# Value products of a head pair in one go from the second batch on, and the fifth chunk of the products with U on four column tiles

## The chip, the cores and the metric

The kernel runs on one core of a Trainium2 chip. A core has a matrix engine (TensorE; PE in the profile, with its loads of the stationary operand shown apart as PEld), a vector engine (VectorE, DVE), a scalar engine (ScalarE, ACT), GpSimd (POOL) and SyncE (SP), which here starts most transfers. The metric is the device time of one execution in microseconds (us), lower is better; the time quoted is the median of several executions.

## What is computed

Attention that keeps only the scores within tau of a row's largest, then a channel mixing block with a low-rank mixing along the sequence, then a mixture of eight experts. The part that the change touches is the value product of the attention and the low-rank mixing:

```python
batch, n_heads, seq, head_dim = 4, 8, 576, 64
scores = scale * np.matmul(q, k.transpose(0, 1, 3, 2))
attn = masked_softmax(scores, tau)
out = np.matmul(attn, v)                 # value products
...
xt = x.transpose(0, 2, 1)                # (batch, 512, 576)
h = xt @ U @ V                           # U: 576 x 32, V: 32 x 576
u = x + h.transpose(0, 2, 1)
ch = np.maximum(u @ w_ch1, 0.0) @ w_ch2
x = u + ch                               # then gating and experts
```

## The kernel before

The four batches (b = 0 to 3) go one after another. In each, the eight heads are taken as four pairs (hp = 0 to 3), and the 576 query rows of a pair as five groups (g = 0 to 4): groups 0 to 3 are 128 rows of both heads, group 4 is the last 64 rows of both. `front` makes the scores of a group, their maxima, exponentials, mask and norm; `back` turns the group's probabilities round with PE transposes into PSUM tiles `tp` (L416, L422), which ACT copies to `ptt` (L417, L423, L424). Batch 0 runs alone (`attention_alone`). From batch 1 on the attention of batch b is interleaved with the channel block of batch b-1 (`channel`, whose matmuls are lines L698 to L700 and L713 to L715), by cost numbers that the generators yield. These only order the code: a list scheduler of the framework then sets the order of each engine by priority and by when it believes operands and buffers to be ready.

The 576 query rows of a pair have two halves: columns 0 to 255 (groups 0 and 1) and 256 to 575 (groups 2 to 4), each with its own `ptt`. The value products of a half write one PSUM tile `po`: four pairs of matmuls with 64 stationary columns each, L435 for the first head into the upper 64 partitions and L436 for the second into the lower 64, and then one matmul with 128 stationary columns, L439, for the last key chunk of both heads. They stand in `back` behind group 1 for the first half and behind group 4 for the second. ACT copies `po` to `xT` (L442), and a chain of small steps is appended, `chain`: transposes of that half into chunks (`tx`, L461), copies of the chunks to `xsd` (L463 by DVE; the fifth chunk, 64 rows, by ACT in L472, or L475 in batch 0), and, for the second half alone, the products with U (`tT`, L484), a replication (L490) and the products with V (L499 or L506). The products with U are five matmuls, one for each chunk, with 32 stationary columns each. Chunk c writes partitions 32·(c mod 4) on, so that chunks 0 to 3 lie on four column tiles of the array, and chunk 4 lies on the first one again.

All matmuls whose operands are plain float32 run as two passes, and the trace shows both. From batch 1 on the PSUM tag `tp` has two buffers, which `tp`, `po`, `tx`, `tT` and the tiles after them share (`po_tile`); scores have two buffers of their own (`s`) and the channel block two (`mm`).

A stretch, below, is a run of matmuls on PE with fewer than 128 stationary columns (L435 and L436, L484, and the gating logits L751), between matmuls with the whole width. Transposes with a 64-partition output are not among them. In the program's order for PE there are 76 stretches before: 40 of value products, 26 of products with U and 10 of logits.

Of the kernel before, what the change touches and what calls it, by code (L numbers as in the profile page):

```python
# [14 lines left out]
AF = mybir.ActivationFunctionType  # L15
# [32 lines left out]
HALVES = ((0, 256), (256, 320))  # L48
# [35 lines left out]
SCALED = 1  # L84
# [19 lines left out]
def attention_channel_moe(ctx, tc, qk, vv, tau, umat, vrep, wch, wgl, wexp, consts, out):  # L104
    nc = tc.nc
    pe, dve, act, pool, sp = nc.tensor, nc.vector, nc.scalar, nc.gpsimd, nc.sync
# [11 lines left out]
    u_sb = cp.tile([128, 5 * RK], F32, name="u_sb")  # L118
# [30 lines left out]
    def bank(tag, shape, name):  # L149
        return BANKS["pool"].tile(shape, F32, tag=tag, name=name, bufs=BANKS["bufs"][tag])  # L150
# [17 lines left out]
    def po_tile(name):  # L168
        return bank("po" if "po" in BANKS["bufs"] else "tp", [128, 512], name)
# [81 lines left out]
    u_flat, u_sb = u_sb, u_sb.rearrange("p (c r) -> p c r", c=5)  # L251
# [143 lines left out]
    def back(b, hp, g, inp, G):  # L395
        pt, rvs = G.pt, G.rvs
        nm = f"{b}_{hp}_{g}"
        last = g == 4
        v = inp[3]
        src = pt.rearrange("p a b -> p (a b)")  # L400
        half = g // 2 if g < 4 else 1
        o, n = HALVES[half]
        if g in (0, 2):
            if half == 0 and b == 0 and hp % 2:

                PT[0] = mlp.tile([128, 9, n], F32, tag="yT1", name=f"ptt{nm}")
            else:
                PT[0] = ap.tile([128, 9, n], F32, tag=f"ptt{half}", name=f"ptt{nm}", bufs=1)
        ptt = PT[0]
        q0 = g * 128 - o  # L410
        if not last:
            for c0 in range(0, 9, 4):
                m = min(4, 9 - c0)
                tp = bank("tp", [128, 4, 128], f"tp{nm}_{c0}")
                for c in range(c0, c0 + m):
                    pe.transpose(tp[:, c - c0], src[:, c * 128:c * 128 + 128], ident)  # L416
                act.activation(ptt[:, c0:c0 + m, q0:q0 + 128], tp[:, :m], AF.Copy)  # L417
                yield 0.11 * m
        else:
            tp = bank("tp", [128, 4, 128], f"tp{nm}")  # L420
            for c in range(4):
                pe.transpose(tp[:, c], src[:, c * 128:c * 128 + 128], ident)  # L422
            act.activation(ptt[:, 0:4, 256:320], tp[:, :, :64], AF.Copy)  # L423
            act.activation(ptt[:, 5:9, 256:320], tp[:, :, 64:], AF.Copy)  # L424
            tp = bank("tp", [128, 2, 128], f"tpr{nm}")
            pe.transpose(tp[:64, 0], src[:, 512:576], ident)
            pe.transpose(tp[:, 1], src[:, 448:576], ident)
            act.activation(ptt[:64, 4, 256:320], tp[:64, 0, :64], AF.Copy)
            act.activation(ptt[64:, 4, 256:320], tp[64:, 1, 64:], AF.Copy)
            yield 0.65  # L430
        if g not in (1, 4):
            return
        po = po_tile(f"po{nm}")
        for j in range(4):
            pe.matmul(po[:64, :n], lhsT=v[:, j * 64:j * 64 + 64], rhs=ptt[:, j], start=(j == 0), stop=False)  # L435
            pe.matmul(po[64:, :n], lhsT=v[:, 384 + j * 64:448 + j * 64], rhs=ptt[:, 5 + j], start=(j == 0), stop=False)  # L436
            if b == 0:
                yield 0.6
        pe.matmul(po[:, :n], lhsT=v[:, 256:384], rhs=ptt[:, 4], start=False, stop=True)  # L439
        xT = rows_of(b)  # L440
        xu = xT[:, hp, o:o + n]
        act.activation(xu, po[:, :n], AF.Copy)  # L442
        CHAIN.append(chain(nm, hp, half, xT, xu, rvs if b < SCALED else None))
        if b:
            yield 2.4

    def chain(nm, hp, half, xT, xu, rvs):

        o, n = HALVES[half]
# [4 lines left out]
        xsd = XS[0]  # L454
# [24 lines left out]
            next(conv)  # L479
        pst = po_tile(f"tT{nm}")[:, :128]  # L480

        for c in range(5):
            r = 32 * (c % 4)
            pe.matmul(pst[r:r + 32], lhsT=u_sb[:, c], rhs=xsd[:, c], start=(c < 4), stop=(c not in (0,)))  # L484
        tT = ap.tile([128, 128], F32, tag="tT", name=f"tT{nm}", bufs=1)
        act.activation(tT, pst, AF.Copy)
        yield 0.7
# [19 lines left out]
            act.activation(u, pu[:, :n], AF.Copy)  # L507
            yield 0.45

    PT, XS, RV, CHAIN = [None], [None], [None], []  # L510

    def link():

# [13 lines left out]
    def rows_of(b):  # L527

        if b not in X:
            for _ in STORE.pop(b - 2, ()):  # L530
                pass
            X[b] = mlp.tile([128, 4, S], F32, tag=f"yT{b % 2}", name=f"yT{b}")
        return X[b]
# [354 lines left out]
    early, first, cap, jump, n1, base0, base1, most, key, pos, over, t1, t2 = (ex1[:, i] for i in range(13))  # L888
# [482 lines left out]
```

## Time and profile before

| | us |
|---|---|
| median of 3 runs | 1046.02 (1045.58 to 1048.26) |
| the profiled execution | 1037.89 |
| its span, first to last instruction | 1036.1 |
| PE busy in it | 1001.9 (97%) |
| DVE, ACT, POOL busy | 717.5, 625.4, 134.3 |

A row of the list of groups or of the timeline is: line, engine, operation, output tile, input tiles, shape and count. The start that the trace gives for a matmul is when its data begin to stream; its end lies after the start of the next one, since matmuls overlap in the pipeline. So what a matmul costs on PE is read from the distance of two starts, not from its duration. A share of busy time near 100% on PE says that hardly any time is left in which it waits; it does not say that the array works at its best in that time.

### The profile page before, as it was taken

The numbers are of one execution on the slowest core, as the hardware profiler recorded it, in microseconds if no ns is written. First come the engines' busy times: TensorE is split into PE (matmuls) and PEld (weight loads), VectorE is DVE, ScalarE is ACT, GpSimd is POOL, SyncE is SP. The second block draws the span as 40 slices with busy tenths as digits, with TensorE's granted clock in tenths as the row PEclk, the third lists the DMA queues.
The fourth block names the chain that finished last, engine by engine and source line by source line (L and its number), as shares of the span: only waits on it lengthen the run. The fifth ranks groups of instructions, "written<-read, shape, count | busy, mean of one in ns | idle before, by whom it ended". The sixth has DMA issues, their size and how long they took to land. (4 is left out here: it accounts for less than half of the span.)

```text
span 1036.1 us, 17665 instructions
## 1 busy us (share of the span) xinstructions
PE 1001.9 (97%) x6256; PEld 836.1 (81%) x6256; DVE 717.5 (69%) x1761; ACT 625.4 (60%) x1270; POOL 134.3 (13%) x115
## 2 busy tenths in 40 slices
PE   7898999999999999999999999999999999999996
PEld 4666677767677787788888898999998988889984
DVE  7988676877668878686776664583378855566673
ACT  6888877886677767767574653422354334455562
POOL 1331133231000000000000000004410321111100
PEclk9999999999999999999999999999999999999999
DMA  6745477865332322422121110354055565555650
GB/s 211 229 141 158 156 238 237 259 207 170 104 112 85 110 76 93 134 78 83 59 85 42 42 40 32 128 191 136 20 181 186 169 224 175 171 189 197 202 183 16
DMA packets 58241, 143.71 MB, mean 139 GB/s; under 512 B 7389, under 2 KB 8157, under 8 KB 58144
## 3 DMA queue, kind: packets, MB, share of 16 engines
q1 hardware_dynamic: 54784, 132.27, 39.1%
q0 software_dynamic: 3360, 10.23, 3.0%
q8 instruction: 51, 0.84, 0.3%
q14 instruction: 46, 0.38, 0.1%
HBM read 124.65 MB, written 18.61 MB: 138 GB/s over the span
## 5 line engine op out<-in xcount | busy, mean ns | idle before, releaser
L1121 ACT ACTIVATE eh<-ew 128x512 fp32r<-128x512 f32 x160 | 94.2, 628 | 68.1 <-PE el L1237 44.6
L1122 DVE TENSOR_TENSOR el<-ew,eh 128x512 fp32r<-128x512 f32 x160 | 106.3, 690 | 38.0 <-ACT eh L1121 36.6
L698 PE MATMUL l<-uh,w0h 128*128 128x256 f32 (+2 forms) x352 | 126.6, 360 | 0.7 <-ACT yT L507 0.7
L363 DVE SCALAR_TENSOR_TENSOR p<-s,st,p 128x576 f32<-128x576 f32 x144 | 114.2, 815 | 17.4 <-ACT p L359 13.7
L700 PE MATMUL l<-uh,w0l 128*128 128x256 f32 (+2 forms) x352 | 122.8, 349 | 0.0
L699 PE MATMUL l<-ul,w0h 128*128 128x256 f32 (+2 forms) x352 | 122.5, 348 | 0.0
L359 ACT ACTIVATE p<-s,st 128x576 f32<-128x576 f32 x144 | 103.7, 739 | 28.8 <-DVE st L348 27.5
L348 DVE TENSOR_REDUCE st<-s 128x1 f32<-128x576 f32 x144 | 105.4, 751 | 18.9 <-PE s L315 18.2
L713 PE MATMUL l<-hh,w1h 128*128 128x512 f32 (+3 forms) x320 | 115.5, 361 | 0.0
L714 PE MATMUL l<-hl,w1h 128*128 128x512 f32 (+3 forms) x320 | 113.0, 353 | 0.0
L715 PE MATMUL l<-hh,w1l 128*128 128x512 f32 (+3 forms) x320 | 112.5, 351 | 0.0
L417 ACT ACTIVATE ptt<-tp 128x512 f32<-128x512 f32 (+1 forms) x192 | 88.2, 491 | 30.3 <-PE tp L416 30.1
L313 PE MATMUL s<-kh,qs 128*128 128x288 f32 x320 | 95.2, 318 | 5.3 <-DVE p L363 3.6
L677 POOL TENSOR_TENSOR w1l<-wr,w1h 128x512 fp32r<-128x512 f32 x24 | 31.8, 1335 | 526.4 <-DVE rha L980 428.8
L416 PE MATMUL tp<-cst,p 128*128 128x128 f32 x576 | 91.1, 276 | 6.4 <-ACT ptt L417 6.3
L718 DVE TENSOR_TENSOR yT<-l,yT 128x448 f32<-128x448 f32 (+2 forms) x96 | 50.2, 523 | 59.3 <-PE l L715 58.5
L315 PE MATMUL s<-kl,qs 128*128 128x288 f32 x320 | 89.0, 298 | 0.0
L373 ACT ACTIVATE p<-p,rv 128x576 f32<-128x576 f32 x108 | 78.7, 772 | 15.5 <-DVE rv L380 15.5
L416 PEld LDWEIGHTS tp<-cst,p 128*128 128x128 f32 x576 | 67.6, 140 | 21.7 <-ACT ptt L417 12.8
L675 ACT ACTIVATE w1h<-wr 128x512 fp32r<-128x512 f32 x64 | 38.4, 628 | 60.9 <-PE l L714 56.6
L313 PEld LDWEIGHTS s<-kh,qs 128*128 128x128 f32 x320 | 60.5, 189 | 15.4 <-issue 6.6
L436 PE MATMUL po<-ptt,v 128*64 128x256 f32 (+1 forms) x256 | 70.7, 414 | 2.0 <-ACT ptt L417 2.0
(600 smaller groups left out, 2476.6 us busy)
## 6 DMA issues: line engine op xcount, KB each, us to landing
ew<-in_wexp_dram SPq DMA_DIRECT2D x80, 512.0 KB, 4.5
wr<-wdram SPq DMA_DIRECT2D x128, 256.0 KB, 2.9
cr<-in_wch_dram SPq DMA_DIRECT2D x32, 512.0 KB, 5.0
raw<-in_qk_dram SPq DMA_DIRECT2D x30, 304.0 KB, 3.0
wdram<-w SPq DMA_DIRECT2D x32, 256.0 KB, 2.8
v<-in_vv_dram SPq DMA_DIRECT2D x16, 352.0 KB, 3.4
raw<-in_qk_dram SPq DMA_DIRECT2D x16, 320.0 KB, 3.1
raw<-in_qk_dram SPq DMA_DIRECT2D x17, 288.0 KB, 3.1
```

Of the source, the lines that this page charges most:

```text
L313: pe.matmul(s["t"][:, h, :288], lhsT=qs[:, qc:qc + 128], rhs=kh[:, k0:k0 + 288], start=(j == 0), stop=False)
L348: dve.tensor_reduce(out=self.st[:, 0, h:h + 1], in_=self.t[h], axis=AX.XY, op=ALU.max, negate=True)
L359: act.activation(self.halves(h), self.t[h], AF.Exp, bias=self.st[:, 0, h:h + 1])
L363: dve.scalar_tensor_tensor(out=p, in0=self.t[h], scalar=self.st[:, 1, h:h + 1], in1=p, op0=ALU.is_ge, op1=ALU.mult, accum_out=self.rvs[:, ...
L416: pe.transpose(tp[:, c - c0], src[:, c * 128:c * 128 + 128], ident)
L698: pe.matmul(pm, lhsT=w1h[:, wk], rhs=uh[k], start=(k == 0), stop=False)
L699: pe.matmul(pm, lhsT=w1h[:, wk], rhs=ul[k], start=False, stop=False)
L700: pe.matmul(pm, lhsT=w1l[:, wk], rhs=uh[k], start=False, stop=(k == 3))
L713: pe.matmul(pm, lhsT=w2h[:, wd], rhs=xh, start=(f == f0), stop=False)
L714: pe.matmul(pm, lhsT=w2h[:, wd], rhs=xl, start=False, stop=False)
L715: pe.matmul(pm, lhsT=w2l[:, wd], rhs=xh, start=False, stop=(f == f0 + 3))
L1122: dve.tensor_tensor(out=lo, in0=x, in1=hi.bitcast(F32), op=ALU.subtract)
```

## The change

From batch 1 on, `back` does nothing behind group 1 but transposes, and behind group 4 it issues the value products of both halves: first the eight 64-column matmuls of the first half, then those of the second, and then the two 128-column matmuls. Both `po` tiles, that is both buffers of `tp`, are in use at once; the copies by ACT and the two chains follow. The cost yielded is 4.8 in one piece rather than twice 2.4. Batch 0 keeps its halves apart. In all batches the products with U begin with chunk 4 on the first column tile, then chunks 2, 3 and 0 on the others, and chunk 1 is cut into four matmuls of 32 columns, one on each column tile, which complete the sums: eight matmuls where there were five.

```diff
@@ back @@
-        if g not in (1, 4):
+        if g not in (1, 4) or b and g == 1:
             return
-        po = po_tile(f"po{nm}")
-        for j in range(4):
-            pe.matmul(po[:64, :n], lhsT=v[:, j * 64:j * 64 + 64], rhs=ptt[:, j], start=(j == 0), stop=False)
-            pe.matmul(po[64:, :n], lhsT=v[:, 384 + j * 64:448 + j * 64], rhs=ptt[:, 5 + j], start=(j == 0), stop=False)
-            if b == 0:
-                yield 0.6
-        pe.matmul(po[:, :n], lhsT=v[:, 256:384], rhs=ptt[:, 4], start=False, stop=True)
+        halves = (0, 1) if b else (half,)
+        pos = [po_tile(f"po{nm}_{x}") for x in halves]
+        for x, po in zip(halves, pos):
+            n, ptt = HALVES[x][1], PTS[x]
+            for j in range(4):
+                pe.matmul(po[:64, :n], lhsT=v[:, j * 64:j * 64 + 64], rhs=ptt[:, j], start=(j == 0), stop=False)
+                pe.matmul(po[64:, :n], lhsT=v[:, 384 + j * 64:448 + j * 64], rhs=ptt[:, 5 + j],
+                          start=(j == 0), stop=False)
+                if b == 0:
+                    yield 0.6
+        for x, po in zip(halves, pos):
+            n = HALVES[x][1]
+            pe.matmul(po[:, :n], lhsT=v[:, 256:384], rhs=PTS[x][:, 4], start=False, stop=True)
...
+        for x, po in zip(halves, pos):
+            o, n = HALVES[x]
+            xu = xT[:, hp, o:o + n]
+            act.activation(xu, po[:, :n], AF.Copy)
+            CHAIN.append(chain(f"{nm}_{x}", hp, x, xT, xu, rvs if b < SCALED else None))
         if b:
-            yield 2.4
+            yield 4.8
@@ chain @@
-        for c in range(5):
-            r = 32 * (c % 4)
-            pe.matmul(pst[r:r + 32], lhsT=u_sb[:, c], rhs=xsd[:, c], start=(c < 4), stop=(c not in (0,)))
+        for r, c in zip((0, 32, 64, 96), (4, 2, 3, 0)):
+            pe.matmul(pst[r:r + 32], lhsT=u_sb[:, c], rhs=xsd[:, c], start=True, stop=False)
+        for r in (0, 32, 64, 96):
+            pe.matmul(pst[r:r + 32, r:r + 32], lhsT=u_sb[:, 1], rhs=xsd[:, 1, r:r + 32], start=False, stop=True)
```

The lines of `back` move by up to ten: in the changed kernel the value products are L439, L440 and L446, their copies L451, `tx` is L470, and the products with U are L492 and L494.

PE, batch 3, third pair (`po_2_...`): the value products of the first half before, with what follows them up to their transposes `tx`.

```order
L698 MATMUL l_2_9_0_6431<-uh_4880,w0h_9_6069 128x448
L699 MATMUL l_2_9_0_6431<-ul_4881,w0h_9_6069 128x448
L435 MATMUL po_2_1_6387<-ptt_2_0_6256,v_5561 64x256
L436 MATMUL po_2_1_6387<-ptt_2_0_6256,v_5561 64x256
...
L439 MATMUL po_2_1_6387<-ptt_2_0_6256,v_5561 128x256
L700 MATMUL l_2_9_0_6431<-uh_4880,w0l_9_6070 128x448
L698 MATMUL l_2_9_0_6431<-uh_4880,w0h_9_6069 128x448
L699 MATMUL l_2_9_0_6431<-ul_4881,w0h_9_6069 128x448
L461 MATMUL tx_2_1_6398<-cst,yT_5352 128x128 x2
```

The second half of that pair stands 113 rows later, alike. The same pair in the changed kernel, from the last rows of the first half on:

```order
L439 MATMUL po_2_4_0_6644<-ptt_2_0_6289,v_5521 64x256
L440 MATMUL po_2_4_0_6644<-ptt_2_0_6289,v_5521 64x256
L439 MATMUL po_2_4_1_6645<-ptt_2_2_6467,v_5521 64x320
L440 MATMUL po_2_4_1_6645<-ptt_2_2_6467,v_5521 64x320
...
L446 MATMUL po_2_4_0_6644<-ptt_2_0_6289,v_5521 128x256
L446 MATMUL po_2_4_1_6645<-ptt_2_2_6467,v_5521 128x320
L470 MATMUL tx_2_4_0_6666<-cst,yT_5627 128x128 x2
L708 MATMUL l_2_11_0_6684<-uh_4916,w0h_11_6588 128x448
```

Two stretches became one of sixteen matmuls, and `tx` of the first half stands right behind the last `po` matmul, with no matmul of the channel block between. It is so in 10 of the 12 pairs; in the other two one such matmul stands between.

PE, end of batch 1, last pair: the products with U before. In 5 of the 16 pairs (three in batch 0, the last one of batch 1 and of batch 2) they stand in three stretches, as here.

```order
L461 MATMUL tx_3_4_3038<-cst,yT_1544 64x128
L484 MATMUL tT_3_4_3061<-xsd_0_1_364,u_sb 32x128 x2
L714 MATMUL l_0_12_0_0_3090<-hl_12_2695,w1h_12_2599 128x512
L715 MATMUL l_0_12_0_0_3090<-hh_12_2694,w1l_12_2600 128x512
L713 MATMUL l_0_12_0_0_3090<-hh_13_2927,w1h_13_2690 128x512
L714 MATMUL l_0_12_0_0_3090<-hl_13_2928,w1h_13_2690 128x512
L484 MATMUL tT_3_4_3061<-xsd_0_1_364,u_sb 32x128 x2
L715 MATMUL l_0_12_0_0_3090<-hh_13_2927,w1l_13_2691 128x512
L713 MATMUL l_0_12_0_0_3090<-hh_14_2995,w1h_14_2923 128x512
L484 MATMUL tT_3_4_3061<-xsd_0_1_364,u_sb 32x128
```

And after, at the same place:

```order
L470 MATMUL tx_3_4_1_3076<-cst,yT_1771 64x128
...
L724 MATMUL l_0_12_0_0_3114<-hl_13_2973,w1h_13_2702 128x512
L492 MATMUL tT_3_4_1_3082<-xsd_0_1_0_364,u_sb 32x128 x4
L494 MATMUL tT_3_4_1_3082<-xsd_0_1_0_364,u_sb 32x32 x4
L725 MATMUL l_0_12_0_0_3114<-hh_13_2972,w1l_13_2703 128x512
L723 MATMUL l_0_12_0_0_3114<-hh_14_3042,w1h_14_2968 128x512
L724 MATMUL l_0_12_0_0_3114<-hl_14_3043,w1h_14_2968 128x512
L500 MATMUL rep_3_4_1_3093<-tT_3_4_1_3091,cst 128x128
```

All eight stand in one piece there, as in all 16 pairs. Over the whole program 51 stretches are left of 76: 25 of value products (13 in batch 0, 12 in batches 1 to 3, where there were 14 and 26), 16 of products with U (4 and 12, where there were 10 and 16) and the 10 of logits. The scheduler also lays the rest of batches 1 to 3 anew: exponentials, copies and channel matmuls stand in a somewhat different order on all engines.

## Rows read from the trace of the kernel before

**Rows 1.** Busy time by stage: part of batch 0, then batches 1 to 3.

```profile
core 0: us, PE busy (x) PEld busy (x) DVE busy (x) ACT busy (x) POOL busy (x), PEclk, DMA share, GB/s
...
28.00:56.00 28.00, 24.16 (x163) 17.41 (x162) 25.66 (x67) 23.38 (x50) 12.30 (x10) 1.00 0.66 213
...
113.00:285.00 172.00, 164.15 (x930) 123.94 (x928) 126.42 (x268) 133.17 (x264) 41.25 (x31) 1.00 0.62 197
285.00:460.00 175.00, 174.40 (x1033) 135.82 (x1030) 134.96 (x334) 127.49 (x254) 0.00 (x0) 1.00 0.30 98
460.00:640.00 180.00, 179.92 (x1223) 159.04 (x1222) 118.86 (x303) 110.56 (x227) 0.00 (x0) 1.00 0.18 59
```

**Rows 2.** Timeline of PE, a value-product stretch: start, duration, what.

```profile
625.16 0.28 PE L698 MATMUL l<-uh,w0h 128*128 128x256 f32 x1
625.28 0.28 PE L699 MATMUL l<-ul,w0h 128*128 128x256 f32 x1
625.49 0.48 PE L435 MATMUL po<-ptt,v 128*64 128x320 f32 x1
625.49 0.48 PE L436 MATMUL po<-ptt,v 128*64 128x320 f32 x1
625.81 0.43 PE L435 MATMUL po<-ptt,v 128*64 128x320 f32 x1
...
626.08 0.43 PE L435 MATMUL po<-ptt,v 128*64 128x320 f32 x1
...
627.42 0.43 PE L435 MATMUL po<-ptt,v 128*64 128x320 f32 x1
...
627.79 0.81 PE L439 MATMUL po<-ptt,v 128*128 128x320 f32 x2
...
628.55 0.28 PE L698 MATMUL l<-uh2b,w0h 128*128 128x256 f32 x1
```

**Rows 3.** Timeline, products with U in one stretch, batch 3.

```profile
633.71 0.62 PE L484 MATMUL tT<-xsd,u_sb 128*32 128x128 f32 x10
...
634.26 0.47 PE L713 MATMUL l<-hh,w1h 128*128 128x448 f32 x1
```

**Rows 4.** Timeline of PE, second of three stretches of products with U, batch 2.

```profile
436.94 0.40 PE L713 MATMUL l<-hh,w1h 128*128 128x512 f32 x1
437.17 0.40 PE L714 MATMUL l<-hl,w1h 128*128 128x512 f32 x1
437.50 0.41 PE L484 MATMUL tT<-xsd,u_sb 128*32 128x128 f32 x4
437.84 0.51 PE L715 MATMUL l<-hh,w1l 128*128 128x512 f32 x1
438.18 0.39 PE L713 MATMUL l<-hh,w1h 128*128 128x512 f32 x1
```

**Rows 5.** Timeline, from the last value product to its transposes, ACT free.

```profile
608.64 0.70 PE L439 MATMUL po<-ptt,v 128*128 128x256 f32 x2
...
609.38 0.38 ACT L442 ACTIVATE yT<-po 128x256 f32<-128x256 f32 x1 [2.64 <-PE po L439]
...
609.82 0.32 PE L461 MATMUL tx<-cst,yT 128*128 128x128 f32 x1
```

**Rows 6.** The same on PE in batch 1, ACT behind.

```profile
192.84 0.81 PE L439 MATMUL po<-ptt,v 128*128 128x320 f32 x2
...
195.65 0.44 PE L461 MATMUL tx<-cst,yT 128*128 128x128 f32 x2 [0.95 <-ACT yT L442]
```

**Rows 7.** PE's waits in batch 1 (113 to 285 us): total us, times, longest.

```profile
PE po L436 <- ACT ptt L417: 1.3, 1, 1.3
...
PE po L435 <- ACT ptt L417: 0.9, 1, 0.9
```

**Rows 8.** Timeline, short matmuls (10 columns, 128 stationary columns) in the last channel block.

```profile
698.63 0.51 PE L963 MATMUL pia<-rha,r1a 96*128 96x10 f32 x4
...
699.00 0.36 PE L698 MATMUL l<-uh,w0h 128*128 128x256 f32 x1
```

More of the change, by code (lines that the diff above doesn't have):

```diff
@@ L408, in back @@
                 PT[0] = ap.tile([128, 9, n], F32, tag=f"ptt{half}", name=f"ptt{nm}", bufs=1)
+            PTS[half] = PT[0]
         ptt = PT[0]
@@ L430, in back @@
             yield 0.65
-        if g not in (1, 4):
+        if g not in (1, 4) or b and g == 1:
             return
-        po = po_tile(f"po{nm}")
-        for j in range(4):
-            pe.matmul(po[:64, :n], lhsT=v[:, j * 64:j * 64 + 64], rhs=ptt[:, j], start=(j == 0), stop=False)
-            pe.matmul(po[64:, :n], lhsT=v[:, 384 + j * 64:448 + j * 64], rhs=ptt[:, 5 + j], start=(j == 0), stop=False)
-            if b == 0:
-                yield 0.6
-        pe.matmul(po[:, :n], lhsT=v[:, 256:384], rhs=ptt[:, 4], start=False, stop=True)
-        xT = rows_of(b)
-        xu = xT[:, hp, o:o + n]
-        act.activation(xu, po[:, :n], AF.Copy)
-        CHAIN.append(chain(nm, hp, half, xT, xu, rvs if b < SCALED else None))
+        halves = (0, 1) if b else (half,)
[11 more added lines that the diff above has]
+            pe.matmul(po[:, :n], lhsT=v[:, 256:384], rhs=PTS[x][:, 4], start=False, stop=True)
+        xT = rows_of(b)
+        for x, po in zip(halves, pos):
[3 more added lines that the diff above has]
+            CHAIN.append(chain(f"{nm}_{x}", hp, x, xT, xu, rvs if b < SCALED else None))
         if b:
-            yield 2.4
+            yield 4.8
     def chain(nm, hp, half, xT, xu, rvs):
@@ L508, in chain @@
             yield 0.45
-    PT, XS, RV, CHAIN = [None], [None], [None], []
+    PT, PTS, XS, RV, CHAIN = [None], {}, [None], [None], []
     def link():
```

## The prediction, made before the changed kernel was run

> **What bounds the kernel now.** I read the busy time by stage first. In batches 2 and 3 PE is busy for 174.40 of 175 and 179.92 of 180 us, in batch 1 for 164.15 of 172, at a granted clock of 1.00 (the 2.4 GHz level) [rows 1]. No other engine passes 135 of 175 there. So a microsecond that PE saves in batches 1 to 3 is a microsecond of the kernel, unless PE then waits for something. Batch 0 is different: in the stretch shown DVE is busy for 25.66 of 28 us and PE for 24.16, filler matmuls included, so PE's savings there reach the end only in part. The stages after batch 3 are not changed; they move as a whole.
>
> The second view is PE's timeline, read by distances of starts. Inside a value-product stretch the two heads start together and a pass of 320 columns takes 0.27 us (625.81 to 626.08). The edges cost more [rows 2]. The channel matmul before the stretch starts at 625.28; one of its size takes 0.12 (625.16 to 625.28), but the stretch starts after 0.21: 0.09 lost. The first pass takes 0.32 and not 0.27: 0.05 lost. On the way out L439 starts 0.37 after the last pass rather than 0.27: 0.10 lost. Then L439's two passes and one 256-column matmul take 0.76 to 628.55, where 2 × 0.27 + 0.12 = 0.66 is work: 0.10 lost. A stretch costs 0.34 us by its edges alone, whatever is in it. All 76 stretches have such edges, so their number is what I count.
>
> **The change part by part.** The profiled execution took 1037.89 us, 1.8 over its span; the median of the three runs is 1046.02, 8.1 above it. I make the sum against 1037.89 and take the same microseconds off the median.
>
> (1) Value products, batches 1 to 3: 26 stretches become 12. The matmuls are the same in number and size, so only edges go: 14 × 0.34 = 4.8 us, on PE's path. Nothing lies between the halves in the new order, and the step from 256 to 320 columns inside a stretch is an ordinary one.
>
> (2) Products with U that were split. One stretch takes 0.55 us to the next matmul [rows 3]. In the split form one part takes 0.34 (437.50 to 437.84), entered 0.33 after a matmul that takes 0.23 (0.10 lost) and followed by one that takes 0.34 instead of 0.23 (0.11 lost) [rows 4]. Three parts of 0.34 are 1.02, against 0.55: 0.47 more, and two further entries and exits, 2 × 0.21 = 0.42. That is 0.89 for each split group. Two are in batches 1 and 2: 1.8 us. Chunk 4 first means that the group waits for its last copy at the head, so that it does not have to be broken up.
>
> (3) The fifth chunk, 12 groups in batches 1 to 3. The 0.55 is the edge (some 0.12) and four rounds of 0.11: two passes of four chunks side by side, then two passes of chunk 4 alone on one tile [rows 3]. The last two rounds, 0.22, become two rounds of four matmuls of 32 columns. By columns a round would be a quarter, 0.03; at worst the eight passes go one after another. The nearest row for short matmuls is L963, with 10 columns but 128 stationary ones: four passes take 0.37 (698.63 to 699.00), 0.09 each [rows 8]. Eight of those are 0.74, a loss of 0.52 a group. I take 0.07 for both rounds, near the quarter, because chunks on different tiles do start together today (ten passes fit into 0.55) and only 32 stationary columns are loaded. So 0.15 × 12 = 1.8 us gained; the bounds are a gain of 1.9 and a loss of 6.2.
>
> The Trainium skill (TensorEngine Tiling, Instruction Overhead) speaks against this part: a matmul has about 60 cycles of overhead, one with a single column takes as long as one with 60, and a tiling factor is not to be taken from a dimension that is already small. No row here has short matmuls on four tiles; that result is the third rival below.
>
> (4) The wait that is added. `tx` of the first half needs ACT's copy of `po`. With ACT free, `tx` starts 1.18 us after the start of L439 (608.64 to 609.82), and before the change channel matmuls fill that time [rows 5]. Now only L446 of both halves fills it: 0.32 and 0.21 for the first half's two passes, 2 × 0.27 for the second's, 1.07 together. The rest, 0.11, is a stall, with the whole of PE's queue behind it, channel and scores alike: 10 × 0.1 = 1.0 us lost; where one channel matmul of 0.23 stands between, none.
>
> (5) Waits that may go. In batch 1 PE waits 1.3 and 0.9 us for a copy of `ptt` right before value products [rows 7]. The first half now needs no recent copy and covers those of the second. I count nothing: the new order can lose as much elsewhere. Bounds: 2.2 gained, 3 lost.
>
> (6) Batch 0: three split groups (3 × 0.89), one split value product less (0.34), four shorter fifth chunks (4 × 0.15): 3.6 us on PE. Since DVE is the busier engine there, I take a third, 1.2, with bounds 0 and 3.6.
>
> The copies by ACT, their sizes, the transfers and the two chains are the same in number; ACT and DVE have over 40 us of slack in each of batches 1 to 3 bar ACT's 39 in the first [rows 1], which hides their new order. Should that cover fail, it is rival four.
>
> Sum: 4.8 + 1.8 + 1.8 - 1.0 + 1.2 = 8.6 us off: 1029.3 for a profiled execution, **1037.4** as a median.
>
> **The rivals.** *More than that:* batch 0 passes all of its 3.6 on and the waits of (5) vanish: 8.6 + 2.4 + 2.2 = 13.2 off, 1032.8. For it speaks that those waits have their cause exactly where the order changed; against it, DVE's load in batch 0.
>
> *The gain is eaten by the new order.* The scheduler lays three batches anew, and batch 1 already has 7.85 us in which PE is not busy [rows 1]. If that doubles, 0.7 is left: 1045.3, no change to be seen. Against it: batches 2 and 3, with the same planning, have 0.7 together.
>
> *Short matmuls go in turn:* each of the eight short passes takes half of a 128-column pass, 0.055, one after the other, 0.44 in all where 0.22 was. Then (3) is a loss of 0.22 instead of a gain of 0.15, 12 × 0.37 = 4.4 worse: 1041.8.
>
> *Slower: ACT comes late to the copy.* ACT works in order, and in batch 1 one copy came so late that `tx` started 2.81 us after L439 (192.84 to 195.65), 0.95 of it as a bare wait [rows 6]. The new order puts `tx` right behind `po`, so such a delay would now stand in full: 2.81 - 1.07 = 1.7 a pair. In all twelve pairs that is 20.9 against the 9.6 that the rest saves: 1057.3. The gain is gone from 0.8 us a pair on, and the kernel visibly slower from 1.06. Against it: in batches 2 and 3 PE's total idle time is too small for such delays to be common.
>
> That the change does not do what it says I leave out: the program's order already has the 51 stretches, and the edges are paid on the engine alone.
>
> **How the numbers follow.** The forecast, 1034 to 1041 around 1037.4, has 0.70; more than that 0.07; short matmuls in turn 0.07; eaten 0.10; slower 0.06. A measurement of this kernel can tell about 0.3%, 3.1 us, from no change. The first three are faster by more than that: 0.84. Eaten is the same, 0.10. Slower 0.06. The range takes in the first three and the upper tail of the forecast: 1032 to 1043.5.
>
> **What would show it.** PE's order on the chip with 12 value-product stretches in batches 1 to 3, each entered with 0.09 lost and left with 0.20, and 0.27 at the seam of the halves; no `tT` stretch over 0.42 us to the next matmul (about 0.40 if (3) holds, 0.77 if short matmuls go in turn); a wait of `tx` for the copy near 0.1 and not near 1; batches 1 to 3 shorter by about 7.4 us together, batch 0 by 0 to 3.6. The prediction is wrong if the stretches are merged and these batches do not get shorter, or if PE's idle time in them grows by more than 4 us.

## The result, and the profile after

The changed kernel takes 1050.54 us (median of 14 runs, 1046.58 to 1056.62), the kernel before 1045.1 beside it (14 runs, 1042.41 to 1048.26): a ratio of 1.0053, 95% interval 1.0035 to 1.0072. It is slower by half a per cent; 1037.4 had been forecast. The profiled execution took 1051.68, its span 1049.9.

Busy time by the same stretches as [rows 1], columns as there:

```profile
28.00:56.00 28.00, 24.08 (x169) 17.33 (x167) 26.39 (x63) 23.00 (x49) 11.06 (x10) 1.00 0.65 208
113.00:285.00 172.00, 159.53 (x942) 123.30 (x943) 126.66 (x265) 132.27 (x263) 42.15 (x31) 0.97 0.63 196
285.00:460.00 175.00, 173.48 (x1040) 133.87 (x1039) 132.12 (x317) 124.26 (x247) 0.00 (x0) 1.00 0.30 96
460.00:640.00 180.00, 179.39 (x1240) 158.80 (x1238) 118.29 (x313) 113.12 (x226) 0.00 (x0) 1.00 0.19 60
```

In batch 1 PE is idle for 12.47 us, where it was 7.85, and its granted clock is 0.97 where it was 1.00. In batches 2 and 3 it is idle for 2.1 us, where it was 0.7. The waits of batch 1 are others than in [rows 7] (waiting instruction, releaser, us in total, times, longest); first PE's, then ACT's, from 115 to 285 us, those with the longest single wait of each list:

```profile
PE s L313 <- DVE p L363: 4.8, 3, 3.3
PE tp L417 <- ACT ptt L418: 3.4, 2, 2.3
PE tp L417 <- ACT p L373: 1.7, 3, 0.7
PE tx L470 <- ACT yT L451: 0.6, 1, 0.6
```

```profile
ACT p L359 <- DVE st L348: 7.3, 4, 4.1
ACT top L212 <- DMA cr<-in_wch_dram: 5.3, 3, 2.5
...
ACT w0h L685 <- DMA wr<-wdram: 2.2, 1, 2.2
```

The 1.3 and 0.9 us ahead of value products are gone, as step (5) had thought possible. In their place stand longer waits of scores for masks (L363, DVE) and of group transposes for copies to `ptt` (ACT).

**The edges went as forecast.** PE's timeline of a merged stretch in batch 2 (start, duration, what), to be read beside [rows 2]:

```profile
323.57 0.40 PE L725 MATMUL l<-hh,w1l 128*128 128x512 f32 x1
323.90 0.43 PE L439 MATMUL po<-ptt,v 128*64 128x256 f32 x1
...
325.46 0.38 PE L439 MATMUL po<-ptt,v 128*64 128x256 f32 x1
...
325.67 0.43 PE L439 MATMUL po<-ptt,v 128*64 128x320 f32 x1
...
327.56 0.43 PE L439 MATMUL po<-ptt,v 128*64 128x320 f32 x1
...
327.93 1.24 PE L446 MATMUL po<-ptt,v 128*128 128x256 f32 x4
329.10 0.44 PE L470 MATMUL tx<-cst,yT 128*128 128x128 f32 x2
329.29 0.48 PE L723 MATMUL l<-hh,w1h 128*128 128x512 f32 x1
...
332.14 0.30 PE L313 MATMUL s<-kh,qs 128*128 128x288 f32 x1
```

It is entered 0.33 us after a matmul of 0.23 (0.10 lost), crosses from one half to the other in an ordinary step (325.46 to 325.67), and is left 0.37 after the last pass (0.10 lost). The products with U, beside [rows 3], take 0.41 us to the next matmul instead of 0.55, and stand in one piece in all pairs:

```profile
339.66 0.43 PE L492 MATMUL tT<-xsd,u_sb 128*32 128x128 f32 x8
339.90 0.24 PE L494 MATMUL tT<-xsd,u_sb 128*32 128x32 f32 x8
340.07 0.50 PE L724 MATMUL l<-hl,w1h 128*128 128x512 f32 x1
```

**What the merged stretch leaves the others.** ACT and DVE beside the same stretch (in brackets the idle time before, and what ended it):

```profile
326.17 1.44 ACT L373 ACTIVATE p<-p,rv 128x576 f32<-128x576 f32 x2 [1.37 <-DVE rv L380]
328.66 0.38 ACT L451 ACTIVATE yT<-po 128x256 f32<-128x256 f32 x1 [1.05 <-PE po L446]
...
333.85 1.38 ACT L359 ACTIVATE p<-s,st 128x576 f32<-128x576 f32 x2 [4.21 <-DVE st L348]
```

```profile
329.58 0.42 DVE L472 COPY xsd<-tx 128x256 f32<-128x256 f32 x1 [2.73 <-PE tx L470]
332.34 0.62 DVE L728 TENSOR_TENSOR yT<-l,yT 128x448 f32<-128x448 f32 x1 [2.34 <-PE l L725]
```

From 323.90 to 332.14 PE makes value products and then channel matmuls; no scores come, and ACT and DVE idle for some 5 us each. Their work then comes in a heap. In batch 2 PE hardly waits for it. In batch 1 there are longer waits. There ACT first waits for loads of weights (top, w0h), and the copy to `ptt` behind them comes late:

```profile
155.57 0.79 ACT L212 ACTIVATE top<-cr 128x512 f16<-128x512 bf16 x1 [2.51 <-DMA cr<-in_wch_dram]
158.55 0.63 ACT L685 ACTIVATE w0h<-wr 128x512 fp32r<-128x512 f32 x1 [2.18 <-DMA wr<-wdram]
159.09 0.72 ACT L359 ACTIVATE p<-s,st 128x576 f32<-128x576 f32 x1
160.45 0.78 ACT L212 ACTIVATE top<-cr 128x512 f16<-128x512 bf16 x1 [0.64 <-DMA cr<-in_wch_dram]
161.10 0.57 ACT L418 ACTIVATE ptt<-tp 128x512 f32<-128x512 f32 x1
```

PE at that place:

```profile
159.00 0.40 PE L725 MATMUL l<-hh,w1l 128*128 128x512 f32 x1
161.73 0.66 PE L417 MATMUL tp<-cst,p 128*128 128x128 f32 x4 [2.33 <-ACT ptt L418]
...
162.45 0.39 PE L724 MATMUL l<-hl,w1h 128*128 128x512 f32 x1
162.68 0.40 PE L725 MATMUL l<-hh,w1l 128*128 128x512 f32 x1
...
163.53 0.63 PE L725 MATMUL l<-hh,w1l 128*128 128x512 f32 x1
163.95 0.63 PE L723 MATMUL l<-hh,w1h 128*128 128x512 f32 x1
...
188.64 0.61 PE L313 MATMUL s<-kh,qs 128*128 128x288 f32 x1 [3.34 <-DVE p L363]
...
190.43 0.63 PE L709 MATMUL l<-ul,w0h 128*128 128x512 f32 x1
190.86 0.63 PE L710 MATMUL l<-uh,w0l 128*128 128x512 f32 x1
```

PE waits 2.33 us, runs on with 0.23 us for 512 columns (162.45 to 162.68), and from 163.53 on needs 0.42: the granted clock, 1.00 from 161.7 to 163.1, is 0.50 from 163.2 to 166.5, so it has gone from 2.4 to 1.2 GHz. At 188.64 scores have waited 3.34 us for a mask, and the matmuls behind take 0.43 again, at 0.50 from 188.7 to 192.0. DVE ahead of that mask (L363):

```profile
186.18 1.54 DVE L294 SCALAR_TENSOR_TENSOR qs<-raw,t,qs 64x608 fp32r<-64x608 f32 x1 [1.19 <-ACT qs L292]
187.75 0.82 DVE L363 SCALAR_TENSOR_TENSOR p<-s,st,p 128x576 f32<-128x576 f32 x1
```

It stood behind a copy of q for the next pair, which had waited for ACT. Waits like these two and the clock behind them are the two parts of what batch 1 loses: measured by stages, as in the experiments below, it takes 167.4 us instead of 162.7 in these two profiles, with PE idle for 11.2 us instead of 6.7 and a mean clock of 0.97 instead of 1.00.

### The profile page after: what moved, and what is told of

Read it like the earlier page. It is cut to its first block, busy times and chain, and to the rows that moved or that the text cites. A ratio compares the mean times of both kernels' runs of the same rounds, so it can differ in the third digit from the quotient of the medians.

```text
span 1049.9 us, 17851 instructions
## 1 busy us (share of the span) xinstructions
PE 1004.7 (96%) x6351; PEld 844.3 (80%) x6352; DVE 721.0 (69%) x1761; ACT 627.3 (60%) x1270; POOL 134.4 (13%) x115
## 3 DMA queue, kind: packets, MB, share of 16 engines
q1 hardware_dynamic: 54784, 132.27, 39.7%
## 5 line engine op out<-in xcount | busy, mean ns | idle before, releaser
L363 DVE SCALAR_TENSOR_TENSOR p<-s,st,p 128x576 f32<-128x576 f32 x144 | 114.2, 814 | 13.7 <-ACT p L359 10.3
L313 PE MATMUL s<-kh,qs 128*128 128x288 f32 x320 | 98.5, 326 | 9.6 <-DVE p L363 7.4
L417 PE MATMUL tp<-cst,p 128*128 128x128 f32 x576 | 94.7, 280 | 10.5 <-ACT ptt L418 8.6
L687 POOL TENSOR_TENSOR w1l<-wr,w1h 128x512 fp32r<-128x512 f32 x24 | 32.4, 1362 | 526.7 <-DVE rha L990 426.8
L708 PEld LDWEIGHTS l<-uh,w0h 128*128 128x128 f32 x352 | 67.0, 190 | 7.4 <-DVE hl L712 0.8
L710 PEld LDWEIGHTS l<-uh,w0l 128*128 128x128 f32 x352 | 66.9, 190 | 6.4 <-POOL w0l L687 1.2
```

The lines of the kernel that those rows point to most:

```text
L313: pe.matmul(s["t"][:, h, :288], lhsT=qs[:, qc:qc + 128], rhs=kh[:, k0:k0 + 288], start=(j == 0), stop=False)
L363: dve.scalar_tensor_tensor(out=p, in0=self.t[h], scalar=self.st[:, 1, h:h + 1], in1=p, op0=ALU.is_ge, op1=ALU.mult, accum_out=self.rvs[:, ...
L708: pe.matmul(pm, lhsT=w1h[:, wk], rhs=uh[k], start=(k == 0), stop=False)
L710: pe.matmul(pm, lhsT=w1l[:, wk], rhs=uh[k], start=False, stop=(k == 3))
```

## Experiments

Times are set against the kernel before, run beside each group on the same chip, so a ratio compares across groups and a time does not. Stage times are read from each kernel's profile, from the end of one mixing stage (the copies to `uh`) to the next; "interval" is the time between the value products of the first and of the second pair of batch 1 (the last halves, L439 or L446).

| kernel | ratio, 95% interval | batch 1, us | interval | batches 2 and 3, us |
|---|---|---|---|---|
| before, again | 0.999 (0.9979 to 1.0001) | 161.8 | 39.2 | 360.4 |
| changed, again | 1.005 (1.0031 to 1.0069) | 169.8 | 51.4 | 360.1 |
| merge alone | 1.0074 (1.0059 to 1.009) | 167.9 | 48.4 | 362.9 |
| products with U alone | 0.9954 (0.9939 to 0.9969) | 161.8 | 40.3 | 358.6 |
| the same, again | 0.9948 (0.9934 to 0.9962) | 160.9 | 39.5 | 358.6 |
| changed, merged from batch 2 | 0.9977 (0.9965 to 0.999) | 161.9 | 40.1 | 359.7 |
| the same, chain later | 0.9956 (0.9941 to 0.9971) | 161.4 | 39.7 | 358.8 |
| changed, merged in batch 1 only | 1.003 (1.0017 to 1.0043) | 169.9 | 51.1 | 358.8 |
| changed, `top` on GpSimd | 1.0102 (1.0082 to 1.0122) | 171.5 | 45.5 | 360.1 |
| changed, conversion earlier | 1.0065 (1.005 to 1.008) | 168.5 | 47.4 | 360.1 |
| products with U alone, conversion earlier | 0.9982 (0.9969 to 0.9995) | 164.2 | 41.4 | 358.6 |
| changed, cost spread | 1.0002 (0.9986 to 1.0017) | 162.2 | 40.0 | 359.3 |
| cost in one piece, no merge | 0.9995 (0.9977 to 1.0013) | 161.1 | 41.0 | 359.8 |
| changed, cost spread, chain later | 0.9987 (0.9973 to 1.0) | 167.1 | 44.6 | 358.1 |
| the same, conversion earlier | 0.9994 (0.9984 to 1.0005) | 168.2 | 48.5 | 358.3 |
| changed, second pair of batch 1 apart | 1.0008 (0.9992 to 1.0023) | 161.9 | 45.2 | 360.1 |

The stage is that of one execution, the ratio a median of 5 to 12. The kernels with spread cost, with the cost in one piece and with the second pair apart had their profile in one of their shortest runs (1038.1 of 1038.1 to 1045.8, 1037.2 of 1036.0 to 1045.5, 1040.3 of 1037.4 to 1043.6), so their stages look better than their medians. The two with spread cost and a later chain had it in their longest (1043.62 of 1036.95 to 1043.62, 1045.43 of 1039.24 to 1045.43) and the changed kernel, again, in one of its longest (1048.95 of 1042.73 to 1049.97), so theirs look worse. What separates short and long stages of batch 1 shows in all these profiles: where it took up to 162.7 us, the clock in it was 1.00 throughout and PE idle for 5.6 to 9.4 us; where it took 164.2 or more, the mean clock was 0.96 to 0.99 and PE idle for 8.9 us or more.

**1. The two halves of the change, and both kernels again.** The merge alone has the five old matmuls of L484; the products with U alone leave `back` as before:

```diff
-        for r, c in zip((0, 32, 64, 96), (4, 2, 3, 0)):
-            pe.matmul(pst[r:r + 32], lhsT=u_sb[:, c], rhs=xsd[:, c], start=True, stop=False)
-        for r in (0, 32, 64, 96):
-            pe.matmul(pst[r:r + 32, r:r + 32], lhsT=u_sb[:, 1], rhs=xsd[:, 1, r:r + 32], start=False, stop=True)
+        for c in range(5):
+            r = 32 * (c % 4)
+            pe.matmul(pst[r:r + 32], lhsT=u_sb[:, c], rhs=xsd[:, c], start=(c < 4), stop=(c not in (0,)))
```

Before, again:

> The kernel before, unchanged, with the granted clock of every execution. Theory A (the change's new waits cost time and drop TensorE's clock): the mean granted clock stays at 0.995 or above in most executions, and the median is within 2 us of 1045. Theory B (the half-clock windows and the waits for instructions in the expert stage come and go from execution to execution, whatever the kernel): the clock lies between 0.983 and 0.998 here too, and the time falls with it by some 10 us per 0.01.

Changed, again:

> The changed kernel again. Theory A: ratio to before 1.003 to 1.008, in the trace the waits of batch 1 (the transposes of L417 for copies by ACT, 2.1 to 2.5 us each) stand at the same places, and half-clock windows follow them. Theory B: the places differ from the first profile, some windows are gone, and the two stalls of the expert stage (3.3 us on PE and 4 us on ACT) are gone or elsewhere.

Merge alone:

> The value products of a pair in one go from batch 1 on, the products with U as before. Theory A (the merge makes the waits): the loss is all here, 1.004 to 1.009, because the gain of the products with U (1.8 + 1.8 us by my sum) is missing and the new waits remain. Theory C (the short matmuls of the products with U are what costs): this half gains its 3.8 us, 0.996. Theory B: 0.997 to 1.003.

Products with U alone:

> The products with U with chunk 4 first and the fifth chunk over four column tiles, the value products as before. Theory A: a gain, as the sum of the prediction has it for this part, 3.6 us in batches 1 to 3 and up to 3.3 in batch 0, 0.994 to 0.997. Theory C (short matmuls go one after the other): a loss of 2 to 4 us, 1.002 to 1.004. Theory B: 0.997 to 1.003.

Measured: 1039.41, 1045.3, 1047.42 and 1035.26 us, the kernel before 1040.5. So theory A holds for where the loss is: the merge alone loses 6.9 us, the products with U gain 5.2, and on top of them the merge costs 10.0. In batch 1 the changed kernel's profile is 8.0 us longer than that of the products with U alone: PE is idle for 12.6 us instead of 7.3, and busy for 157.2 instead of 154.6 at a mean clock of 0.97 instead of 1.00. Idle time is thus two thirds of it; the rest is busy time that got longer at the lower clock. Theory C falls. Theory B is right in part: the kernel before has clocks of 0.992 to 0.997 here, so it is not at full clock either, but the changed kernel's are lower on the whole (0.986 to 0.993), and its waits of batch 1 stand at the same places again, 3.6 us for `ptt` at 164 and 3.3 for a mask at 192. One thing was of the first profile alone: stalls in the expert stage, PE's 3.3 us with nothing shown that it waits for among them, and a lower clock (0.99 instead of 1.00) make that stage 262.7 us there, and 256.5 in the second profile (255.8 in the kernel before). They make 6 of the 14 us between the two first profiles and did not come again here, where the ratio is the same.

The stretch of 55 us in batch 1 where the two part, columns as in [rows 1], first the kernel before, then the changed one:

```profile
150.00:205.00 55.00, 51.35 (x300) 38.28 (x300) 41.73 (x87) 43.30 (x84) 16.82 (x13) 1.00 0.77 247
```

```profile
150.00:205.00 55.00, 46.81 (x253) 34.58 (x250) 35.88 (x67) 39.14 (x72) 15.28 (x11) 0.91 0.72 221
```

PE is idle for 8.2 us instead of 3.7, and the clock is 0.91. In the second row no engine is near its limit, DMA neither. It is order and waiting, not load.

**2. Which batches.** Merged from batch 2 on, and in batch 1 only (the same edit with `b == 1`):

```diff
-        if g not in (1, 4) or b and g == 1:
+        if g not in (1, 4) or b > 1 and g == 1:
...
-        halves = (0, 1) if b else (half,)
+        halves = (0, 1) if b > 1 else (half,)
...
-            yield 4.8
+            yield 4.8 if b > 1 else 2.4
```

> As the changed kernel, but the value products are merged only from the third batch on (b = 2 and 3); batch 1 keeps its halves apart. Reference point: the kernel with the new products with U alone came to 0.9954. Theory D (the merge loses in batch 1 alone, and gives in batches 2 and 3 what the sum says, 8 x 0.34 saved and 0.8 paid for waits of tx): 0.9937. Theory E (in batches 2 and 3 too, new waits take more than the edges give, as their stages in the trace with the merge alone hint, 1.1 and 1.5 us longer): 0.997 to 0.998. Neither: 0.9954.

> As the changed kernel, but merged only in batch 1. Theory D: all of the merge's loss is here, some 7 us above the kernel with the new products with U alone, 1.002 to 1.003, with waits of PE of 1.5 us and more in batch 1 and a half-clock stretch behind them. Theory E: only a part, about 5 us above, 1.0005. If the waits come from what the whole program's order does and not from the merge in batch 1: near 0.9954.

Measured: 0.9977 and 1.003. The first is as theory E had it, the second as theory D: batch 1 takes 169.9 us instead of 161.8 and is by far the greater loss, but in batches 2 and 3 too the merge gains nothing (359.7 against 358.6 without it). By the ratios the merge costs 0.0076 in batch 1 and 0.0023 in batches 2 and 3, against 0.0096 for both together.

Where the gain goes there can be counted. For every matmul of batches 2 and 3 (the second profiles of before and changed), the time from when its columns should be through (512 columns in 0.23 us, twice for two passes) to the next start, summed by place:

| us lost | before | products with U alone | changed |
|---|---|---|---|
| edges of value products | 5.35 | 5.35 | 3.21 |
| edges of products with U | 1.86 | 1.57 | 1.62 |
| `tx` right behind a value product | 0 | 0 | 0.80 |
| other ways into `tx` | 1.35 | 1.35 | 0.02 |
| into the group transposes | 1.93 | 1.62 | 2.72 |
| between channel and score matmuls | 8.37 | 8.49 | 10.65 |
| the rest | 4.28 | 4.59 | 5.75 |

The eight pairs save 2.1 us at their edges, 0.27 each. The wait of `tx` takes 0.80 and gives 1.33 back elsewhere. Then 4.4 us more than with the products with U alone are lost between matmuls that the change does not touch. Two waits of channel matmuls for `hl`, which DVE writes, are 1.1 of them (0.6 and 0.5); the rest is spread over many steps that each lose little. That these are the heap behind the merged stretch is what the idle ACT and DVE above suggest; it is read, not tested.

**3. The wait of `tx`.** Merged from batch 2, the chain handed on half of the cost later, so that channel matmuls stand between in 5 of 8 pairs:

```diff
-        xT = rows_of(b)
+        xT, links = rows_of(b), []
...
-            CHAIN.append(chain(f"{nm}_{x}", hp, x, xT, xu, rvs if b < SCALED else None))
+            links.append(chain(f"{nm}_{x}", hp, x, xT, xu, rvs if b < SCALED else None))
+        if b > 1:
+            yield 2.4
+        CHAIN.extend(links)
         if b:
-            yield 4.8 if b > 1 else 2.4
+            yield 2.4
```

> As the kernel merged from the third batch on, but the chain of both halves is handed on half of the cost (2.4) later, so that in 5 of the 8 pairs channel matmuls stand between the value products and tx. Theory D and E alike expect that the wait of tx for ACT's copy, 0.1 each, goes in these five pairs: 0.5 us less than the kernel without the delay. Theory E in a stronger form (the merge costs since the chain comes late as a whole): 1 us or more longer than without the delay.

Measured: 0.9956 against 0.9977. In the table's terms the wait fell from 0.79 to 0.30 us, as expected, and batches 2 and 3 from 359.7 to 358.8. The rest of the 2.2 us is not explained by these stages; between the two profiles batch 0, which the edit does not touch, differs by 2.0, at a mean clock of 0.957 and 0.985. The merge is now even with leaving it out, and not better.

**4. Are the loads of the weights the cause?** `top` on GpSimd, so that ScalarE does not wait for `cr`:

```diff
-                tc.keep_in_program_order(act.activation(
+                tc.keep_in_program_order(pool.tensor_copy(
...
-                    raw[:, 4:4 + 4 * m].bitcast(BF16).rearrange("p (n q) -> p n q", q=4)[:, :, 0], AF.Copy))
+                    raw[:, 4:4 + 4 * m].bitcast(BF16).rearrange("p (n q) -> p n q", q=4)[:, :, 0]))
```

> The changed kernel, with the first step of the weight conversion (the copies of cr to top, L212) on GpSimd instead of ScalarE, so that ScalarE's queue no longer stands behind loads of cr. Theory F (the loss of batch 1 is ScalarE waiting in order for cr and wr ahead of the copies of ptt, 3.2 and 1.6 us before PE's wait of 3.6): that wait of PE goes, the half-clock stretch at 164 us too, batch 1 becomes 4 to 8 us shorter and the ratio comes to 0.997 to 1.001. Rival (PE waits since a merged pair holds both buffers of tp and the copies bunch up, whatever ScalarE waits for): 1.004 to 1.006 as before, with the waits of PE on the copies of ptt as long.

Measured: 1.0102, worse. ACT's and PE's waits in batch 1 of this kernel:

```profile
ACT p L359 <- DVE st L348: 11.3, 7, 3.9
ACT w0h L685 <- DMA wr<-wdram: 10.8, 3, 4.5
ACT p L373 <- DVE rv L380: 10.5, 9, 4.1
```

```profile
PE s L313 <- DVE p L363: 6.1, 3, 4.7
PE tp L417 <- ACT p L373: 4.6, 3, 2.5
PE tp L423 <- ACT p L373: 2.9, 2, 2.3
```

PE's waits for `ptt` did go, from 5.1 us to 1.3, and the half-clock stretch at 164 with them. But ACT then waits for the next load, `wr`, and PE for masks and norms. Theory F falls as the cause of the whole, with a reservation: the edit also loads GpSimd, which is busy for 61.4 us of batch 1 instead of 42.0 and also makes the low parts of the weights (L687). Next, the conversion asked for earlier, with the merge and without:

```diff
-        beside = {1: [((1.0 for _ in conv), 30.0)],
+        beside = {1: [((1.0 for _ in conv), 45.0)],
```

> The changed kernel with the weight conversion of batch 1 asked for earlier (its share in the interleaving 45 and not 30, so its steps come about a seventh earlier in the order of ScalarE). Theory K (batch 1's loss is PE waiting behind copies that ScalarE does late, since in its order loads of weights stand ahead that have not landed): with the loads earlier, the waits of ScalarE for cr and wr fall from 8 us to under 4, batch 1 gets 4 us shorter or more, 0.998 to 1.002. Theory L (ScalarE and VectorE bunch their work up behind a merged pair, and the loads only happen to stand there): 1.004 to 1.007 as before.

> The same earlier conversion with the value products as before the change and the new products with U: the reference for the run before it. Both theories: within 2 us of the kernel with the old conversion (0.993 to 0.997); if the earlier conversion is itself a loss or a gain, the run before has it too.

Measured: 1.0065 and 0.9982, 0.0083 apart, against 0.0096 with the old conversion. ACT's waits for these loads fell from 8.3 us to 5.1, not under 4 (`cr` from 6.7 to 5.1; `wr`, 1.6, went), PE's waits for `ptt` from 5.1 to 1.6, and batch 1 stayed at 168.5; the longest wait of PE is now 4.1 us, of scores for a mask. Theory K falls, with the reservation that the waits for `cr` were only shortened by a quarter. Last, the whole conversion drawn out ahead of batch 1 in the program:

```diff
+    for _ in conv:
+        pass
     BANKS.pop("stack").close()
     MM.append(ctx.enter_context(tc.tile_pool(name="mmp", bufs=1, space=PSUM, side="right")))
```

> The changed kernel, with the whole conversion of the channel weights done at the end of batch 0, so that batch 1 has none of its loads, copies (ScalarE), joins (VectorE) and stores. The whole run gets longer by the conversion, which PE then waits for, some 40 to 80 us; what counts is the time of the stage of batch 1 beside its twin without the merge. Theory M (the merge loses in batch 1 because the conversion's work and loads stand in ScalarE's and VectorE's queues there): batch 1 within 1.5 us of the twin, as batches 2 and 3 are, and no wait of PE over 1.5 us in it. Theory L (a merged pair starves and then bunches ScalarE's and VectorE's work, whatever else they have): 5 us or more longer than the twin.

> The twin: the new products with U, value products as before the change, and the whole conversion at the end of batch 0. Its stage of batch 1 is the reference; by the load that goes it should be shorter than 161 us, by 0 to 6 us. Theory M and theory L differ in the distance to the run before it, not in this one.

Measured: 1.0173 (1.0146 to 1.02) and 1.0198 (1.0165 to 1.023). The test did not become what it should: the scheduler laid the conversion into the first 60 us of batch 1, which took 180.5 us with the merge and 188.3 without. What can be read from it, from three runs of each: where the conversion fills the first 60 us the merge costs nothing, the sign even turns; and from the value products of the second pair on, with the conversion through, the two need 84 and 83 us (starting at 213.9 and 221.4). So the merge has no fixed price in batch 1; it depends on what stands beside it. Which of its neighbours decides it, these runs leave open.

**5. The piece of 4.8 or the merged matmuls?** All pairs merged with the cost yielded as before; and the cost moved without any merge (against the products with U alone; the chain of the first half thereby comes one piece later):

```diff
+        if b and g == 1:
+            yield 2.4
         if g not in (1, 4) or b and g == 1:
             return
...
-            yield 4.8
+            yield 2.4
```

```diff
-        if b:
-            yield 2.4
+        if b and g == 4:
+            yield 4.8
```

> The changed kernel in all its matmuls, but the cost of the value products is yielded as before the change: 2.4 behind group 1, where nothing is issued now, and 2.4 behind group 4, not 4.8 in one piece. Theory G (the piece of 4.8 lets the channel block and the weight conversion run ahead in bursts, which find weights not yet loaded, and batch 1 loses by that): most of batch 1's 8 us comes back, 0.996 to 0.999. Theory H (the merged products themselves, which hold both buffers of tp for 5 us, make batch 1's waits): as the changed kernel, 1.004 to 1.006.

> The value products of each half where they were before the change, the new products with U, and only the cost moved: nothing yielded behind group 1, 4.8 behind group 4 (the chain of the first half thereby comes one piece later). Theory G: the loss of batch 1 shows without any merged product, 1.001 to 1.004, against 0.9954 with the old costs. Theory H: 0.995 to 0.997.

Measured: 1.0002 and 0.9995. Each falls between its two theories: against the 0.9954 without either, the merge with spread cost loses 0.0048, the cost in one piece without a merge 0.0041, and both together 0.0096. So the loss has two halves of about equal size, which within their intervals add up. Where the second half is lost is not shown: with the cost in one piece and no merge, batch 1 took 161.1 us in its one profile, no longer than without either edit, and batches 2 and 3 took 1.2 us more. The piece of 4.8 shifts the attention against the channel block: with it the first pair's value products come 33 to 36 us into batch 1, with 2.4 and 2.4 after 38. Then the spread cost with a later chain, alone and with the earlier conversion:

> As the kernel with the cost spread as before (2.4 behind group 1, 2.4 behind group 4), and the chain of a pair handed on after half of the second 2.4, in all three batches. Theory G: like the spread kernel and 0.3 to 1 us shorter, since some of the waits of tx for ACT's copy go. Theory H: 1.002 to 1.006.

> All pairs merged, cost spread 2.4 and 2.4, chain half of the second 2.4 later, conversion earlier: the friendliest order for the merge that I know. Theory K: 0.992 to 0.996, as good as the kernel without the merge or better. Theory L: 0.997 to 1.001, as without the earlier conversion.

Measured: 0.9987 and 0.9994. No order that I tried makes the merge in all batches pay. And the second pair of batch 1 kept apart, since the interval before it holds the loss:

```diff
+        whole = b and (b, hp) != (1, 1)
-        if g not in (1, 4) or b and g == 1:
+        if g not in (1, 4) or whole and g == 1:
...
-        halves = (0, 1) if b else (half,)
+        halves = (0, 1) if whole else (half,)
...
-            yield 4.8
+            yield 4.8 if whole else 2.4
```

> The changed kernel, with the second pair of batch 1 alone kept apart (two value products of a half each, 2.4 and 2.4 of cost); the eleven other pairs merged. In all runs that merge batch 1 at a cost of 4.8, the loss stands between the value products of the first and of the second pair, 48 to 51 us against 40. Theory N (the loss is bound to the second pair being merged, beside the densest part of the conversion): this interval comes back to 38 to 42 us, no half-clock stretch after 150 us, 0.996 to 0.999. Theory O (the first pair's merge with its 4.8 in one piece, 3.6 us earlier than before, sets the rest off): the interval stays at 46 or more, 1.002 to 1.006.

Measured: 1.0008, between both. One pair of twelve, with its cost, is worth 0.004, 4 us: the window from 150 to 205 us shows PE busy for 50.40 us in the 55 and a granted clock of 1.00, where the changed kernel has 47.77 and 0.91. The interval is still 45.2 and not 40, so the first pair's early piece has its share.

**The version that beats both** is the one with the new products with U and the old value products; repeated beside others on another chip:

> The new products with U alone, value products as before, once more and beside the others of this group: 0.994 to 0.997 as before, granted clock 0.994 or more in most executions.

Measured: 0.9948 (1036.09 us against 1041.34).

## Why the prediction was wrong

- **The bound** was read rightly: PE sets the end in batches 1 to 3. But it was read as if a microsecond of work saved were the whole question; what PE waits for is set by the order, and the change made a new one.
- **(1), value products**, 4.8 us: right in kind, a little large. 0.27 us a pair was measured in batches 2 and 3, not 0.34, for in two of the eight merged stretches there (the second profile) the first pass waits for its copies, 0.09 and 0.26 us.
- **(2), split groups**, right: all 16 stand in one piece.
- **(3), the fifth chunk**: 0.138 us saved a group, 0.15 forecast. Four passes of 32 columns side by side follow the next four after 28 ns, where 128 columns take 110 to 130; the forecast had 35. The rival of short matmuls that go in turn is out. The Trainium skill (TensorEngine Tiling (Array Packing), Instruction Overhead), with its 60 cycles for a matmul, would give 25 ns a round at 2.4 GHz as an estimate, near what was measured; that four starts 7 ns apart make 28 fits as well, and no run here separates the two.
- (2), (3) and batch 0's share (6) together had 4.8 us; the products with U alone gave 5.2. That the sums meet so closely is in part luck: by stages, batches 1 to 3 got 1.8 and 2.7 us shorter in the two profiles and not 3.6 (batch 1, where PE waits in any case, by 0 and 0.9), and the profiles of batch 0 differ too much in clock (0.94 to 0.99) to tell its share.
- **(4), the wait of `tx`**, right in size: 0.10 in nearly every pair where `tx` follows at once. That other waits into `tx` would go in return (1.33 us in batches 2 and 3) was not seen.
- **(5), waits that may go**, counted as nothing with bounds of 2.2 gained and 3 lost: **this is the step that failed.** The two waits did go. In their place batch 1 got longer by 8 us beside the products with U alone, and batches 2 and 3, which had no term for new waits, lost more than the 2 us that the edges gave (360.1 against 358.6 without the merge). In all the merge, forecast to gain 4.8 - 1.0 us, cost 10.0. I had taken the bound of the loss from waits that the trace of before shows at these places. But a new order makes waits at new places, and the measure would have been what one wait costs (2 to 3.5 us) and how near PE is to one in that batch.
- **"ACT and DVE have 40 us of slack"** was no cover. It is slack in sum; in a stretch of 10 us they stood idle for 5 and were late in the next. The scores have two buffers, `tp` two; that a piece of 5 us on PE outlasts them is how I read it, no run changed the number of buffers.
- **The clock** was in no step. [rows 1] show 1.00 in batches 1 to 3, and I took it as given. Waits of 2 to 3.5 us were followed by half clock, and the mean fell to 0.91 in the 55 us around the second pair.
- **The rivals.** "The gain is eaten by the new order" named the mechanism and the batch; its price, 7.85 us more of idle time, left out the clock and batches 2 and 3. PE's idle time in batch 1 grew by 4.6 us, over the 4 that I had set as the mark for being wrong. My argument against it, that batches 2 and 3 have only 0.7 us idle with the same planning, was no evidence on batch 1. "Slower: ACT comes late to the copy" had the right sign at the wrong place: `tx` waited 0.1.

## What to carry to other kernels

A saving at the edges of work on the busiest engine is worth its sum only if the order around it stays; where an edit makes two pieces into one long one, look first at what the engines that feed on it do meanwhile, and how many buffers lie between. Change the order and the work in separate steps: the half of this change that touched the order least gave about what its sum said. And where a planner interleaves by cost numbers, moving a cost is a change of its own, here by the ratios worth about as much as the merge.

## What the chip showed that was not expected

TensorE's clock goes with a large part of the spread between executions. The kernel before has a wait of 2.18 us for a mask at 15 us in both of its profiles. Around it, columns as in [rows 1], in the first and in the second:

```profile
14.00:24.00 10.00, 6.66 (x44) 4.96 (x44) 9.46 (x23) 8.82 (x17) 2.96 (x2) 1.00 0.64 207
```

```profile
14.00:24.00 10.00, 7.49 (x33) 5.79 (x33) 8.58 (x18) 7.22 (x14) 2.91 (x2) 0.66 0.60 177
```

The same program and the same wait, a clock of 1.00 once and 0.66 once; batch 0 took 115.8 and 119.5 us. The Trainium skill (TensorE: Matmul & The Clock Gate, Part 1) says that a gate sets the clock by how busy the engine was of late, and that how much of a kernel's start is slow differs from run to run; the two profiles agree. Over the runs of one kernel the time follows: with the cost in one piece, from 1036.0 us at a mean clock of 0.994 to 1045.5 at 0.988; 0.006 of the whole is some 6 of these 9.5 us, as an estimate. So a wait of 2 us on TensorE can cost more than its length, and not always the same.
